# A planner that counts a longer time from a slot-list scatter to whatever rests on its landing, with its places set anew

## The chip, the cores and the metric

One core of one Trainium2 chip. The time is device microseconds of one execution; of the kernel before, three runs gave a median of 997.97 us (997.52 to 999.89).

## The reference

Sliding-window attention feeds a mixture of experts. q, k and v are [8, 8, 576, 64] (8 batches, 8 heads, 576 positions, width 64), float32.

```python
scores = q @ k.T / sqrt(64) - slope[h] * |i - j|      # only 0 <= i - j < 128
attn   = softmax(scores) @ v
x      = attn.transpose(0, 2, 1, 3).reshape(4608, 512)
noisy  = x @ w_gate + log1p(exp(x @ w_noise)) * noise   # [4608, 8]
top2   = the two largest of a row; weights = softmax over them
out[t] = sum over its two experts e of weight * (relu(x[t] @ w1[e]) @ w2[e])
```

w1 is [8, 512, 1024], w2 [8, 1024, 512], so each expert serves some 1152 of the 9216 (token, expert) pairs.

## The kernel before, in words

Attention runs batch by batch on TensorE, VectorE (bias and maximum), ScalarE (exponential, evictions) and GpSimd (selects of the window's blocks, L600 and L601). `rows` and `gate` then make a batch's token rows and its gate logits: `row_major` (L786 scales a row tile out of its bank, L794 and L797 store it to xs_dram), and in `gate` the heads' logits are scaled (L832, VectorE) and summed over the heads on GpSimd (L841, L842). `route(b)` chooses the two experts of each of the batch's tokens and gives every pair a slot in its expert's list: a small table `listed` of 80 lines of 64 numbers is built (L941, L942 on VectorE) and added into slots_dram by an indirect DMA that GpSimd issues (`scatter`, L1009), once for each batch. `gates_out` stores the gate values into xs_dram (L1069, L1073).

What reads the lists: expert 0's first 1024 slots are three early blocks (384, 384 and 256 tokens), which may start when batches 0 to 3, 0 to 5 and 0 to 6 are listed (`CUTS` has 3, 5 and 6). `first_ids` loads such a list on SyncE's queue (L1078), turns it into token numbers on VectorE (`clipped`: L1083, L1084, L1044), and GpSimd gathers the tokens (L1337); the rows are split into two half-precision parts, transposed by DMA (L1455), and go through the first expert product (L1463) and the second. The remaining blocks ("second wave") get their lists from `second_ids` (L1873 and on), the output rows are added into the result by scatters (L1724).

The order of the work is made ahead of the launch. `Order` plays the whole kernel through as strands that yield operations with a planned duration and a rank; an engine that is free in the plan takes the waiting operation of least rank, and emits it then. The order of emission is the order of each engine's queue on the chip, SyncE's DMA queue among them. A strand may also wait until a planned time (`yield order.now + 2.5`). The plan carries no semaphores: what waits for what on the chip follows from the data that instructions touch in the order of emission, so an access to slots_dram waits for the landing of every scatter to it that was emitted before. The ranks come from the constants at the top of the file (`SCATTER[b]`, `ROUTE[b]`, `FINE[...]` and so on); a batch is 20 on the scale of routing.

Three places in the plan count the time until a scatter has landed:

- in `route`, a scatter takes the one token of the ring `listing` first, and `landed_list` gives it back 2.1 us after the scatter's planned end: the next batch's scatter can't be emitted before;
- at the end of `route(b)`, 2.5 us behind `sent[b]` (the batch's gate values stored), an early block's list load may begin;
- in `second_ids`, 2.5 us before the lists of the second wave.

The scatter itself is planned at 1.2 us on GpSimd, and 0.2 us (`LAG`) are added behind each operation.

Of the kernel before, what the change touches and what calls it, by code (L numbers as in the profile page):

```python
# [40 lines left out]
WIDE, HALF = 512, 256  # L41
REST = CAP - 2 * WIDE
BLOCKS = tuple(((FROWS, c - FROWS),) if z < NF else ((0, WIDE), (WIDE, WIDE), (2 * WIDE, c - 2 * WIDE)) for z, c in enumerate(CAPS))
ZERO, EMPTY = -868.7, -2
LOAD = 1336.2
VALUES = 522.7
GATE = (586.3, 114.2, 10.8, 223.3, 430.5, 595.2, 1222.1, 914.0)
ROUTE = (342.7, 2091.0, 1245.6, 114.7, 453.4, 734.2, 1823.4, 1585.4)
SCATTER = (825.8, 1619.1, 1254.4, -2580.7, 356.1, -2057.0, -1202.6, 1165.8)
FFN0, FFN1 = -37.1, 674.3  # L50
WEIGHTS = (1547.8, 1129.9)
TOKENS = -408.2
FINE = (-269.6, -67.8, 591.7, 499.2, 364.6, 91.4, -84.0, -165.4, -508.6, -68.4, -409.6, 76.9, 124.7, -71.9, -108.9, -18.6, -921.6, 304.5, 493.5, 400.7, 136.3, 66.3, 526.5, 2.2, 234.2, -476.5, -453.8, -47.5, -184.4, -278.0, 410.0, 13.0, 37.2, 126.9, -246.8, 12.9, -248.7, 24.3, -130.2, 10.5, -211.1, 146.0, -91.2, -314.4, -30.9, 272.5, -306.7, -204.8, -795.2, 68.5, 336.3, -528.3, 344.2, 61.4, -456.9, 111.8, -186.5, -50.6, -10.3, -525.8, -189.2, 13.2, 55.1, 270.0, 177.0, -536.1, 113.3, 36.7, -51.7, -60.8, 589.7, -248.0, -73.3, -88.5, 652.2, -8.9, -517.4, 295.6, 24.0, -285.0, 895.7, 310.8, -678.8, -379.9, -384.9, -317.9, 31.8, 33.5, -239.2, -604.6, -100.3, -134.7, 154.5, -665.9, 43.3, 311.1, 207.6, -18.8, 338.4, -65.9, -144.2, -324.3, 36.8, 219.5, -55.9, -124.3, 200.0, -551.8, 229.5, 106.3, 1.0, 383.8, -156.7, -416.1, -291.1, -190.4, 45.4, -262.7, -141.2, 180.6, -150.6, -450.1, -201.8, 120.2, -203.1, -129.0, 273.6, 32.0, 96.8, -401.0, -263.6, 134.3, -151.3, 504.8, 21.3, -241.5, -6.7, -424.3, -701.9, 780.4, 28.0, 576.4, -208.7, 237.4, -534.3, 273.3, 215.7, 380.0, 228.8, -184.6, 104.7)
STAGE = (855.9, -105.9, 923.9, 172.5, -770.8, 1148.3, 1067.9, 742.9)
MIDDLE = 1144.0
RESULT = 1472.4
SIZES = (1334.5, 424.5, 1529.3)
SOON = -672.8
TIGHT = (1, 5, 7)
QUICK = (5, 7)  # L60
LATE = (2094.9, -890.9, 647.9, 1175.8, 179.1, -270.3, -892.6, -769.0, 507.2, -1321.9, -1248.3, -168.7, -2569.7, -1705.9, -1040.2)
LAG = 0.2
ADD, TWS = 0.34, 5
BEHIND = 11.7
TURN, MARGIN, LATE_BY = (0.3, 0.3), 1.0, 1.0
TURNED = 7e4
SLACK = 0.8
PACE, READ_BY, AHEAD = 1.1, 2.0, 297.8
HELD = 3
SWITCH, NEAR = 0.093, 39.0  # L70
TOP, SOFT, SPLIT = (1.25, 1.25, 0.76), (1.56, 1.56, 0.8), (0.85, 1.35, 0.85)
SP_COST = 0.45
DMA_RATE = 300e3
# [165 lines left out]
def attention_moe(ctx: ExitStack, tc: tile.TileContext, qk_, v, w_gate, w_noise, noise, w1, w2,  # L239
# [13 lines left out]
    order = Order()  # L253
# [100 lines left out]
    def masks():  # L354
# [17 lines left out]

        yield dve(0.14, FINE[0] + -40, lambda: nc.vector.tensor_scalar(ident, rel, 0.0, None, op0=OP.is_equal))
        yield dve(0.14, FINE[1] + -40, lambda: nc.vector.tensor_scalar(before, rel, 0.0, None, op0=OP.is_lt))
        yield dve(0.7, FINE[2] + -40, folded)
        yield dve(0.7, FINE[3] + -40, of_first)
        for g in range(NP):
            for h in (2 * g, 2 * g + 1):
                yield either(0.65, 0.45, FINE[4] + -20 + 5 * g, LATE[9], lambda e, h=h: bias_of(e, h))
            mark(biased[g])  # L380
# [75 lines left out]
    def loads():  # L456

        for k in range(PAIRS):
            rank = 5 * k - LOAD
            t = qks[k] = yield (qkr, FINE[5] + rank)  # L460
            left[k] = len(GROUPS)
# [6 lines left out]
    def all_values():  # L468
        for y in range(2 * B):
            rank = 10 * y - VALUES  # L470
            if y == 0:
# [167 lines left out]
    def unit(u):  # L639
        k, gr = units[u]  # L640
        blocks = GROUPS[gr]
        t = k * NQ + blocks[0]
        r0, r1, r2, r3, r4, r5, r6, r7 = (t + z for z in STAGE)
        last = gr == 2
# [66 lines left out]
    def weighing(k):  # L711
        b, g, y = k // NP, k % NP, k // 2
        t = k * NQ + 1
        r6, r7 = (t + z for z in STAGE[6:])
        yield parted[k]
# [26 lines left out]
    def rows(b, last, t):  # L742
# [3 lines left out]
        nr, nz = 64 if last else 128, len(blocks)  # L746
        rank = t - GATE[b]

# [25 lines left out]
    def row_major(b, i, xu, den, t, done):  # L774

        rank = t - GATE[b]
        rows = 64 if i == 4 else 128
# [27 lines left out]
    def gate(b, blocks, xu, den, t, done):  # L805


        rank = t - GATE[b]
        nz, i = len(blocks), blocks[0]
# [52 lines left out]
    def route(b):  # L862
# [4 lines left out]
        ln, pl = lp[:, 0], lp[:, 1]  # L867
        rank = 20 * b - ROUTE[b]
        V = nc.vector
# [141 lines left out]

        rank = 20 * b + SCATTER[b]
        yield (listing, FINE[63] + rank)
# [2 lines left out]
        yield sent[b]  # L1016
        mark(routed[b])
        mark(over)
        yield order.now + 2.5
        if b in CUTS:  # L1020
            yield from first_ids(first[CUTS[b]], b + 1, rank)

    listing = Ring([0])

    def landed_list():
        yield order.now + 2.1
        put(listing, 0)

    def first_ids(blk, cut, rank):
# [98 lines left out]
    def weight_rank(e, f):  # L1128

        return 1000 + step_of(e) + f - 4 if e else WEIGHTS[0] + WEIGHTS[1] * f  # L1130

# [100 lines left out]
    def say(e):  # L1232
# [6 lines left out]
        yield begun[e - 1]  # L1239
        yield Op((("SP", 1.5, SIZES[2] + step_of(e) - 1),), load)  # L1240
        mark(known[e])
# [296 lines left out]
    def copied(o, t, rank, end, done):  # L1538
        yield end
        yield either(0.33, 0.34, FINE[123] + rank - MIDDLE, LATE[8], lambda e: copy(e, o, t))  # L1540
        yield order.now + SLACK
        mark(done)

    def two_sums(c, y, rank, end, copies, done, u):
# [3 lines left out]
        both = c[:, 0:2].rearrange("p a b -> p (a b)")  # L1548
        yield dve(0.6, FINE[124] + rank - MIDDLE, lambda: nc.vector.tensor_tensor(both, y, both, op=OP.add))  # L1549
        yield order.now + SLACK  # L1550
        mark(done)
        yield dve(ADD, FINE[125] + rank - MIDDLE, lambda: nc.vector.tensor_tensor(c[:, 4], c[:, 0], c[:, 1], op=OP.add))
        mark(u)

    def last_sum(c, at, t, rank, end, ready_, done, whole):
        yield end
        yield ready_
        yield dve(0.34, FINE[126] + rank - MIDDLE, lambda: nc.vector.tensor_tensor(c[:, at], t, c[:, 0], op=OP.add))  # L1558
        put(hbr, whole)
# [68 lines left out]
    def downs(steps):  # L1628
        held = []
        for blk, f, rank in steps:  # L1630
            yield blk.h[f][0]
            if blk.wide:
# [8 lines left out]
                for j, r in blk.tiles:  # L1641
                    end = yield pe(1.3, FINE[136] + rank, lambda: mm2_wide(blk, f, j, [ev[2] for ev in ws]), False)
                    if f == 3:
                        spawn(result(blk, j, r, rank - RESULT, end))
                spawn(after(blk, f, None, end))
                continue
            if blk is second[-1] and f >= 8 - HELD:
                held.append((f, chunks[blk.e, f]))
                yield chunks[blk.e, f][1]
                if f == 7:  # L1650
                    for j, r in blk.tiles:
                        for z, ev in held:
                            end = yield pe(0.655, FINE[137] + rank, lambda: mm2(blk, z, j, r, ev[2]), False)
                        spawn(result(blk, j, r, rank - RESULT, end))
                    for z, ev in held:
# [20 lines left out]
            for j, r in blk.tiles:  # L1676
                end = yield pe(0.655, FINE[140] + rank, lambda: mm2(blk, f, j, r, ev[2]), False)
                if f == 7:
                    spawn(result(blk, j, r, rank - RESULT, end))
            spawn(after(blk, f, ev[2] if blk.last else None, end))  # L1680
# [61 lines left out]
    def first_tokens():  # L1742
        for z, blk in enumerate(first):
            yield from tokens(blk, ranks1[8 * z] - TOKENS)

# [113 lines left out]
        yield dve(1.3, 1130, starts)  # L1859

    def second_ids():
        yield order.now + 2.5
        for q, blk in enumerate(second):
            rank = 1000 + 8 * q - AHEAD
            t = blk.ix = blk.at = yield (ixr, FINE[148] + rank)
            v = lists2[q % 2]
            nt, rem = blk.n // 128, blk.n % 128
            yield known[blk.e]

            def load_ids():  # L1870
                if blk.e < EARLY:
                    r0 = blk.e * EROWS + blk.s0
                    nc.sync.dma_start(v[:, 0:nt], dram(slots, r0, [[1, 128], [128, nt], [1, 1]]))  # L1873
                    if rem:
                        nc.sync.dma_start(v[0:rem, nt], dram(slots, r0 + nt * 128, [[1, rem], [1, 1]]))
                    return
                one_ = slots.rearrange("(e l) c -> e (l c)", e=E)[bass.ds(said[blk.e], 1)]
                s1 = blk.s0 + nt * 128
                if nt:
                    nc.sync.dma_start(v[:, 0:nt], one_[:, blk.s0:s1].rearrange("o (a p) -> p a o", p=128))  # L1880
                if rem:
                    nc.sync.dma_start(v[0:rem, nt], one_[:, s1:s1 + rem].rearrange("o p -> p o"))

            def numbers_():
                if nt:
                    tokens_of(v[:, 0:nt, 0], t.bitcast(F32)[:, 0:nt], spare[:, 0:nt])
                if rem:
                    tokens_of(v[0:rem, nt], t.bitcast(F32)[0:rem, nt:nt + 1], spare[0:rem, nt:nt + 1])

            yield from move(1e4, rank, load_ids)  # L1890
            yield order.now + READ_BY
            yield dve(0.3, FINE[149] + rank, numbers_)
            mark(blk.ids)
            spawn(weights_back(blk, rank))
# [142 lines left out]
```

## Time and profile before

| | |
|---|---|
| median of 3 runs | 997.97 us (997.52 to 999.89) |
| the profiled execution's own time | 997.48 us |
| its span, first to last instruction | 995.7 us |
| mean granted TensorE clock | 0.988 |
| TensorE busy | 951.8 us (96%) |
| VectorE busy | 822.1 us (83%) |
| ScalarE busy | 569.0 us (57%) |
| GpSimd busy | 382.3 us (38%) |
| HBM read and written | 158 GB/s over the span |

Times in the trace are from the span's start; what lies outside the span is 1.8 us. Attention and routing end near 255 us, the expert products fill the rest. Engines are PE (TensorE), PEld (its weight loads), DVE (VectorE), ACT (ScalarE), POOL (GpSimd) and SP (SyncE, which issues most DMAs); POOLq or SPq is such an engine's own instruction queue. L1078 is line 1078 of the kernel. A bracket behind an instruction gives the idle time of its engine before it and what the profile takes for the release; where a wait was for several things the name can be the wrong one.

### The profile page before, as it was taken

The numbers are of one execution on the slowest core, as the hardware profiler recorded it, in microseconds if no ns is written. First come the engines' busy times: TensorE is split into PE (matmuls) and PEld (weight loads), VectorE is DVE, ScalarE is ACT, GpSimd is POOL, SyncE is SP. The second block draws the span as 40 slices with busy tenths as digits, with TensorE's granted clock in tenths as the row PEclk, the third lists the DMA queues.
The fourth block names the chain that finished last, engine by engine and source line by source line (L and its number), as shares of the span: only waits on it lengthen the run. The fifth ranks groups of instructions, "written<-read, shape, count | busy, mean of one in ns | idle before, by whom it ended". The sixth has DMA issues, their size and how long they took to land. (4 is left out here: it accounts for less than half of the span.)

```text
span 995.7 us, 25350 instructions
## 1 busy us (share of the span) xinstructions
PE 951.8 (96%) x9040; PEld 668.4 (67%) x9040; DVE 822.1 (83%) x2813; ACT 569.0 (57%) x1516; POOL 382.3 (38%) x567
## 2 busy tenths in 40 slices
PE   7999899878999999999999999999999999999996
PEld 5777676655556967596768576766767586667753
DVE  8989899888558898797889988989897898889520
ACT  8998789751445656355646454654555374546312
POOL 4456567676333223222342234323313223343013
PEclk9999999988999999999999999999999999999998
DMA  9785688788799897797887688868997989686124
GB/s 327 241 270 184 182 261 245 215 259 215 206 256 213 216 220 151 167 180 210 163 218 172 164 166 222 192 188 132 224 179 188 200 195 242 114 174 133 19 33 52
DMA packets 236976, 188.89 MB, mean 190 GB/s; under 512 B 147696, under 2 KB 190992, under 8 KB 236848
## 3 DMA queue, kind: packets, MB, share of 16 engines
q1 hardware_dynamic: 219504, 148.31, 56.4%
q0 software_dynamic: 17344, 38.94, 21.4%
q8 instruction: 72, 1.18, 0.5%
q14 instruction: 56, 0.46, 0.1%
HBM read 116.24 MB, written 40.71 MB: 158 GB/s over the span
## 5 line engine op out<-in xcount | busy, mean ns | idle before, releaser
L1724 POOL DMA_INDIRECT out_dram<-yo,ix x69 | 123.7, 1793 | 255.1 <-ACT yo L276 178.3
L1620 PEld LDWEIGHTS <-hh 128*128 128x128 f16 x896 | 85.3, 98 | 73.3 <-issue 0.3
L1588 ACT ACTIVATE hh<-bank 128x256 f16<-128x256 f32 (+8 forms) x116 | 40.1, 347 | 142.3 <-PE bank L1463 57.8
L1620 PE MATMUL bank<-w2ha,hh 128*128 128x512 f16 x288 | 109.2, 379 | 0.0
L1620 PE MATMUL bank<-w2la,hh 128*128 128x512 f16 x288 | 109.2, 379 | 0.0
L1620 PE MATMUL bank<-w2ha,hl 128*128 128x512 f16 x288 | 109.2, 379 | 0.0
L1337 POOL DMA_INDIRECT xg<-xs_dram,ix x34 | 41.9, 1231 | 162.4 <-DVE ix L1084 103.2
L563 ACT ACTIVATE p<-p,nm 128x128 f32<-128x128 f32 x256 | 99.1, 394 | 4.2 <-DVE nm L539 4.0
L1489 PEld LDWEIGHTS <-wth 128*128 128x128 f16 x896 | 87.2, 98 | 18.4 <-issue 2.5
L1620 PEld LDWEIGHTS <-hl 128*128 128x128 f16 x448 | 43.8, 98 | 52.8
L1588 ACT ACTIVATE hh<-c 128x256 f16<-128x256 f32 (+1 forms) x82 | 41.6, 520 | 57.7 <-DVE c L1558 54.2
L524 PE MATMUL bank<-qk 64*64 64x192 f32 (+2 forms) x1152 | 61.4, 327 | 9.6 <-DVE nm L539 5.0
L539 DVE CUSTOM_DVE_ANT_0 p<-bank,bias 128x128 f32<-128x128 f32 x288 | 67.1, 285 | 1.4 <-PE bank L577 1.2
L614 PE MATMUL bank<-pT,vraw 128*64 128x128 f32 (+1 forms) x640 | 59.1, 332 | 8.3 <-POOL pT L601 3.8
L1603 DVE SCALAR_TENSOR_TENSOR hl<-bank,hh 128x384 f16<-128x384 f32 (+8 forms) x88 | 31.2, 363 | 42.1 <-ACT hh L1588 35.1
L276 ACT ACTIVATE yo<-bank,gw 128x512 f32<-128x512 f32 (+6 forms) x56 | 38.3, 686 | 46.5 <-PE bank L1620 22.2
L1337 POOL DMA_INDIRECT xp<-xs_dram,ix x35 | 42.1, 1204 | 58.3 <-DVE ix L1084 27.5
L1293 ACT ACTIVATE mraw<-mraw 128x1024 f32<-128x1024 f32 x56 | 58.6, 1048 | 7.4 <-DMA mraw<-in_w_dram 7.4
L1463 PEld LDWEIGHTS <-w1ha 128*128 128x128 f16 x544 | 48.7, 98 | 20.3 <-issue 0.6
L276 ACT ACTIVATE c<-bank 128x256 f32<-128x256 f32 x94 | 35.0, 378 | 47.2 <-PE bank L1489 46.6
L1489 PE MATMUL bank<-xhe,wth 128*128 128x256 f16 x224 | 61.0, 273 | 0.8 <-DVE c L1549 0.4
L1489 PE MATMUL bank<-xhw,wth 128*128 128x256 f16 x224 | 61.0, 272 | 0.6 <-DVE c L1549 0.4
(349 smaller groups left out, 3178.3 us busy)
## 6 DMA issues: line engine op xcount, KB each, us to landing
raw<-in_w_dram SPq DMA_DIRECT2D x144, 256.0 KB
mraw<-in_w_dram SPq DMA_DIRECT2D x56, 512.0 KB
qk<-in_qk_dram SPq DMA_DIRECT2D x32, 576.0 KB
vraw<-in_v_dram SPq DMA_DIRECT2D x16, 640.0 KB
out_dram<-xg SPq DMA_DIRECT2D x10, 1024.0 KB
xs_dram<-x SPq DMA_DIRECT2D x72, 128.0 KB
out_dram<-yo,ix POOLq DMA_INDIRECT x69
xs_dram<-xg SPq DMA_DIRECT2D x1, 1024.0 KB
```

Of the source, the lines that this page charges most:

```text
L276: nc.scalar.activation(o, i, AF.Copy, **kw)
L524: nc.tensor.matmul(s[h][r * 64:r * 64 + 64, o:o + n_ * 64], qk[half, m * 64:m * 64 + 64], blocks_of(qk[half, QW:QW + S], first_, step, n_) ...
L539: nc.vector.tensor_tensor_reduce(out=o, in0=i, in1=by, scale=-0.125, scalar=3.0e38, op0=OP.add, op1=OP.min, accum_out=m)
L563: nc.scalar.activation(pv, pv, AF.Exp, bias=nm[:, z, h:h + 1], scale=-1.0, accum_out=den[:, i, 2 * g + h:2 * g + h + 1])
L614: nc.tensor.matmul(y, t[:, kb, hh:hh + D], w, start=m == 0, stop=m == len(lst) - 1)
L1293: yield act(us, FINE[81] + rank, lambda: nc.scalar.activation(v, v, sum_, accum_out=o))
L1337: nc.gpsimd.indirect_dma_start(out=o, out_offset=None, in_=xs[0:blk.rows], in_offset=bass.IndirectOffsetOnAxis(ap=blk.at[0:r, j:j + 1], ax ...
L1463: nc.tensor.matmul(t[:, 0:blk.n], wp[:, c], x[:, c, 0:blk.n], start=c == 0 and z == 0, stop=c == 3 and z == 2)
L1489: nc.tensor.matmul(t, wp[:, at + kc], xp[:, 2 * o + kc], start=not add and kc + z == 0, stop=kc + z == 3, skip_group_check=add)
L1588: nc.scalar.activation(o, i, AF.Relu)
L1620: nc.tensor.matmul(blk.y[j], h[:, cs], wp, start=a == 0 and z + m == 0, stop=a == 3 and z + m == 3)
L1724: ins = nc.gpsimd.indirect_dma_start(out=out, out_offset=bass.IndirectOffsetOnAxis(ap=blk.ix[0:r, j:j + 1], axis=0), in_=t[0:r], in_offset ...
```

## The change

The two 2.5 and the 2.1 above become 4.8. Beside that nearly all ranks get other values: every constant from ZERO to LATE that the diff shows, AHEAD and NEAR. Sizes, tiles, engines and operations are the same.

```diff
-LOAD = 1336.2
-VALUES = 522.7
-ROUTE = (342.7, 2091.0, 1245.6, 114.7, 453.4, 734.2, 1823.4, 1585.4)
-SCATTER = (825.8, 1619.1, 1254.4, -2580.7, 356.1, -2057.0, -1202.6, 1165.8)
-FFN0, FFN1 = -37.1, 674.3
+LOAD = 1312.0
+VALUES = 521.5
+ROUTE = (344.2, 2070.6, 1239.7, 114.7, 451.0, 720.1, 1799.0, 1587.4)
+SCATTER = (826.8, 1590.9, 1231.4, -2587.1, 341.2, -2034.5, -1202.9, 1158.6)
+FFN0, FFN1 = -37.3, 650.3
...
-STAGE = (855.9, -105.9, 923.9, 172.5, -770.8, 1148.3, 1067.9, 742.9)
+STAGE = (854.4, -105.9, 922.3, 177.9, -775.2, 1103.9, 1074.4, 742.1)
...
-PACE, READ_BY, AHEAD = 1.1, 2.0, 297.8
+PACE, READ_BY, AHEAD = 1.1, 2.0, 259.0
...
-SWITCH, NEAR = 0.093, 39.0
+SWITCH, NEAR = 0.093, 42.4
...
         yield sent[b]
         mark(routed[b])
         mark(over)
-        yield order.now + 2.5
+        yield order.now + 4.8
         if b in CUTS:
             yield from first_ids(first[CUTS[b]], b + 1, rank)
...
     def landed_list():
-        yield order.now + 2.1
+        yield order.now + 4.8
         put(listing, 0)
...
     def second_ids():
-        yield order.now + 2.5
+        yield order.now + 4.8
         for q, blk in enumerate(second):
```

The 151 values of FINE move in the same way, for example its first ones:

```diff
-FINE = (-269.6, -67.8, 591.7, 499.2, 364.6, 91.4, -84.0, ...
+FINE = (-269.0, -55.2, 568.8, 482.6, 393.2, 92.5, -99.1, ...
```

## Rows read from the trace of the kernel before

**Rows 1.** Windows: busy us (instructions) of each engine, granted clock, DMA share, GB/s.
```profile
0.00:250.00 250.00, 219.22 (x3382) 159.14 (x3383) 224.22 (x1248) 192.64 (x782) 152.96 (x337) 0.97 0.78 240
250.00:950.00 700.00, 696.58 (x5392) 487.80 (x5391) 590.00 (x1544) 368.32 (x717) 219.27 (x220) 1.00 0.82 181
```

**Rows 2.** The same windows view, in stretches of 10 us (PE, PEld, DVE, ACT, POOL).
```profile
90.00:100.00 10.00, 9.60 (x151) 7.04 (x147) 9.84 (x49) 6.38 (x31) 4.17 (x8) 1.00 0.57 180
100.00:110.00 10.00, 7.33 (x105) 5.39 (x103) 7.08 (x49) 6.51 (x29) 8.25 (x21) 0.83 0.64 169
...
200.00:210.00 10.00, 8.87 (x116) 6.34 (x116) 8.47 (x62) 5.61 (x18) 7.96 (x17) 0.66 0.99 314
...
220.00:230.00 10.00, 3.54 (x24) 2.00 (x26) 7.17 (x26) 0.66 (x2) 9.36 (x13) 0.69 0.74 191
...
250.00:260.00 10.00, 10.00 (x64) 5.55 (x63) 7.54 (x31) 5.07 (x12) 2.64 (x5) 1.00 0.89 266
```

**Rows 3.** Timeline of GpSimd, 90 to 104 us: start, us, instruction, idle before and releaser.
```profile
92.34 1.68 POOL L1009 DMA_INDIRECT slots_dram<-listed,line_of  x1 [0.33 <-DVE nm L539]
...
99.43 1.46 POOL L1009 DMA_INDIRECT slots_dram<-listed,line_of  x1 [5.37 <-DVE bank L545]
100.37 1.81 POOL L841 TENSOR_TENSOR lt<-lt 128x256 f32<-128x256 f32 x2
...
103.24 0.21 POOL L842 TENSOR_TENSOR lg<-lt 64x16 f32<-64x16 f32 x1
```

**Rows 4.** Timelines of ScalarE and of TensorE, near 104 us.
```profile
103.49 0.24 ACT L872 ACTIVATE u<-lg 128x40 f32<-128x40 f32 x1 [4.07 <-POOL lg L842]
...
104.26 1.05 PE L783 MATMUL bank<-ident,xul 128*64 128x128 f32 x4 [2.67 <-ACT pT L276]
```

**Rows 5.** Timeline of VectorE, near 96 us.
```profile
96.31 0.22 DVE L942 TENSOR_TENSOR listed<-listed,bank 80x64 f32<-80x64 f32 x1
96.45 0.68 DVE L832 TENSOR_TENSOR lt<-bank,den 128x512 f32<-128x512 f32 x1
```

**Rows 6.** Waits of SyncE's queue: us in total, times, longest.
```profile
SPq L1078 <- DMA slots_dram<-listed,line_of: 8.5, 2, 6.4
```

**Rows 7.** Timelines of GpSimd (the scatters) and SyncE (the queue), 180 to 198 us.
```profile
182.15 1.54 POOL L1009 DMA_INDIRECT slots_dram<-listed,line_of  x1 [0.18 <-issue]
...
190.95 1.44 POOL L1009 DMA_INDIRECT slots_dram<-listed,line_of  x1 [0.23 <-DVE rk L878]
...
188.47 0.38 SPq L475 DMA_DIRECT2D vraw<-in_v_dram  x1
188.90 1.32 SPq L1073 DMA_DIRECT2D xs_dram<-gd  x1
196.86 1.28 SPq L1078 DMA_DIRECT2D list<-slots_dram  x3
```

**Rows 8.** Timelines of VectorE, GpSimd and TensorE behind that list load.
```profile
199.91 0.16 DVE L1083 SCALAR_TENSOR_TENSOR ids<-list,spare 128x3 f32<-128x3 f32 x1 [3.33 <-DMA list<-slots_dram]
...
200.75 1.01 POOL L1337 DMA_INDIRECT xg<-xs_dram,cl  x1 [6.16 <-DVE cl L1044]
...
201.13 1.11 PE L577 MATMUL bank<-ident,p 64*128 64x64 f32 x15 [3.19 <-DVE x L786]
```

**Rows 9.** Timelines of GpSimd and SyncE: the last scatter, the third early list.
```profile
255.18 1.52 POOL L1009 DMA_INDIRECT slots_dram<-listed,line_of  x1 [3.90 <-DMA xs_dram<-gd]
...
260.16 0.81 SPq L1078 DMA_DIRECT2D list<-slots_dram  x2
```

**Rows 10.** Timelines of SyncE and TensorE: third block's last transpose and first product.
```profile
283.88 1.22 SPq L1455 DMA_TRANSPOSE xle<-th  x1
...
298.81 0.27 PE L1463 MATMUL bank<-xhe,w1ha 128*128 128x256 f16 x1
```

**Rows 11.** Timeline of TensorE: the first expert product.
```profile
236.72 0.33 PE L1463 MATMUL bank<-xhe,w1ha 128*128 128x384 f16 x1
```

**Rows 12.** Waits of TensorE, 0 to 300 us: in total, times, longest.
```profile
PE bank L524 <- DMA qk<-in_qk_dram: 4.6, 1, 4.6
```

More of the change, by code (lines that the diff above doesn't have):

```diff
@@ L43 @@
 BLOCKS = tuple(((FROWS, c - FROWS),) if z < NF else ((0, WIDE), (WIDE, WIDE), (2 * WIDE, c - 2 * WIDE)) for z, c in enumerate(CAPS))
-ZERO, EMPTY = -868.7, -2
-LOAD = 1336.2
-VALUES = 522.7
-GATE = (586.3, 114.2, 10.8, 223.3, 430.5, 595.2, 1222.1, 914.0)
-ROUTE = (342.7, 2091.0, 1245.6, 114.7, 453.4, 734.2, 1823.4, 1585.4)
-SCATTER = (825.8, 1619.1, 1254.4, -2580.7, 356.1, -2057.0, -1202.6, 1165.8)
-FFN0, FFN1 = -37.1, 674.3
-WEIGHTS = (1547.8, 1129.9)
-TOKENS = -408.2
-FINE = (-269.6, -67.8, 591.7, 499.2, 364.6, 91.4, -84.0, -165.4, -508.6, -68.4, -409.6, 76.9, 124.7, -71.9, -108.9, -18.6, -921.6, 304.5, 493.5, 400.7, 136.3, 66.3, 526.5, 2.2, 234.2, -476.5, -453.8, -47.5, -184.4, -278.0, 410.0, 13.0, 37.2, 126.9, -246.8, 12.9, -248.7, 24.3, -130.2, 10.5, -211.1, 146.0, -91.2, -314.4, -30.9, 272.5, -306.7, -204.8, -795.2, 68.5, 336.3, -528.3, 344.2, 61.4, -456.9, 111.8, -186.5, -50.6, -10.3, -525.8, -189.2, 13.2, 55.1, 270.0, 177.0, -536.1, 113.3, 36.7, -51.7, -60.8, 589.7, -248.0, -73.3, -88.5, 652.2, -8.9, -517.4, 295.6, 24.0, -285.0, 895.7, 310.8, -678.8, -379.9, -384.9, -317.9, 31.8, 33.5, -239.2, -604.6, -100.3, -134.7, 154.5, -665.9, 43.3, 311.1, 207.6, -18.8, 338.4, -65.9, -144.2, -324.3, 36.8, 219.5, -55.9, -124.3, 200.0, -551.8, 229.5, 106.3, 1.0, 383.8, -156.7, -416.1, -291.1, -190.4, 45.4, -262.7, -141.2, 180.6, -150.6, -450.1, -201.8, 120.2, -203.1, -129.0, 273.6, 32.0, 96.8, -401.0, -263.6, 134.3, -151.3, 504.8, 21.3, -241.5, -6.7, -424.3, -701.9, 780.4, 28.0, 576.4, -208.7, 237.4, -534.3, 273.3, 215.7, 380.0, 228.8, -184.6, 104.7)
@@ L54 @@
-STAGE = (855.9, -105.9, 923.9, 172.5, -770.8, 1148.3, 1067.9, 742.9)
[L55 to L58, printed above, removed]
+ZERO, EMPTY = -857.2, -2
+LOAD = 1312.0
+VALUES = 521.5
+GATE = (586.3, 113.9, 26.9, 200.0, 448.9, 600.9, 1223.1, 933.2)
+ROUTE = (344.2, 2070.6, 1239.7, 114.7, 451.0, 720.1, 1799.0, 1587.4)
+SCATTER = (826.8, 1590.9, 1231.4, -2587.1, 341.2, -2034.5, -1202.9, 1158.6)
+FFN0, FFN1 = -37.3, 650.3
+WEIGHTS = (1554.8, 1178.0)
+TOKENS = -434.4
+FINE = (-269.0, -55.2, 568.8, 482.6, 393.2, 92.5, -99.1, -166.4, -509.2, -68.8, -408.6, 72.4, 109.4, -69.4, -83.6, -18.6, -918.7, 304.2, 492.6, 383.7, 127.4, 59.8, 503.2, 2.2, 220.6, -456.1, -467.4, -49.1, -164.0, -278.0, 370.6, 12.3, 81.8, 127.6, -265.1, 12.9, -255.7, 3.1, -129.8, 0.7, -186.7, 145.8, -81.1, -314.4, -31.0, 206.5, -275.3, -226.3, -809.0, 67.5, 311.8, -524.9, 345.8, 66.8, -458.8, 111.2, -181.1, -56.5, 19.8, -502.0, -197.1, 20.3, 5.2, 270.0, 146.6, -529.6, 110.9, 61.7, -32.4, -33.4, 591.2, -237.5, -79.1, -44.4, 621.2, -6.6, -515.8, 298.1, 24.0, -300.5, 907.5, 310.8, -678.6, -384.7, -392.5, -262.7, 24.9, 32.7, -238.1, -604.5, -92.5, -125.8, 153.0, -663.5, 36.2, 281.8, 210.2, -15.3, 296.9, -59.9, -130.1, -324.9, 36.5, 214.1, -55.9, -107.2, 192.8, -551.9, 208.7, 65.1, 1.0, 383.8, -170.1, -414.0, -299.8, -196.5, 49.3, -286.0, -151.4, 180.8, -151.0, -403.1, -211.1, 120.5, -202.3, -149.2, 284.1, 23.9, 24.4, -394.2, -263.2, 89.8, -154.3, 509.6, 25.3, -232.4, -6.7, -421.6, -701.9, 780.5, 23.7, 572.2, -208.6, 246.0, -542.7, 280.7, 232.7, 381.8, 206.0, -193.0, 101.4)
@@ L59 @@
+STAGE = (854.4, -105.9, 922.3, 177.9, -775.2, 1103.9, 1074.4, 742.1)
+MIDDLE = 1141.9
+RESULT = 1487.2
+SIZES = (1360.4, 424.9, 1533.7)
+SOON = -654.8
 TIGHT = (1, 5, 7)
 QUICK = (5, 7)
-LATE = (2094.9, -890.9, 647.9, 1175.8, 179.1, -270.3, -892.6, -769.0, 507.2, -1321.9, -1248.3, -168.7, -2569.7, -1705.9, -1040.2)
+LATE = (2082.6, -896.6, 632.3, 1187.7, 137.0, -269.8, -843.0, -797.9, 507.6, -1324.0, -1233.0, -161.6, -2573.4, -1709.3, -1043.4)
 LAG = 0.2
```

## The prediction

> **What bounds the kernel now.** I read long windows first. From 0 to 250 us TensorE is busy 219.2 us (30.8 idle, mean granted clock 0.97), from 250 to 950 us 696.6 (3.4 idle) [rows 1]. So from 250 us on TensorE sets the pace, and time can go only in attention, gate and routing before it; what is saved there passes to the end if the first expert block starts as much earlier. Ten-microsecond windows show dips: 100 to 110 (TensorE 7.33 busy), 200 to 210 (clock 0.66), and 220 to 230 (3.54 busy), where the last batch drains [rows 2]. In front of the first, VectorE is busy 9.84 of 10; it is the next engine late in this stage, so a dip gives back at most what VectorE lost in it.
>
> Then I asked what the first two dips waited for. The **first** begins on GpSimd: batch 0's list scatter was issued from 92.34 to 94.02, the next one ran only at 99.43, and the sum over heads (L841, L842) stood behind it until 103.45 [rows 3]. ScalarE waited 4.07 us for that sum, its evictions came late, and TensorE stood 2.67 us [rows 4]. The profile names a VectorE line as the releaser of the second scatter; that was not it, since the scatter's own data (L942) was written by 96.53 [rows 5]. The landing is what is left, 5.41 us after the issue's end.
>
> The **second** is on the DMA queue: SyncE's list loads (L1078) waited for scatters 8.5 us in two waits, the longest 6.4 [rows 6]. The queue's record before the load ends at 190.22, the load goes at 196.86. The last scatter ahead of it is the one at 190.95, which is batch 4's: this L1078 loads the first block's list, which wants batches 0 to 3 alone, and batch 3's scatter was at 182.15 [rows 7]. So the landing took 196.86 - 192.39 = 4.47 us. VectorE, with the list's numbers at the head of its queue, stood 3.33 us until 199.91; GpSimd, with the gather at its head, 6.16 us; TensorE 3.19 us, until VectorE got to L786 behind the numbers [rows 8].
>
> A third wait, on the last early list: the load goes at 260.16, 3.46 us after batch 7's scatter ends [rows 9]. TensorE is busy all through 250 to 260 [rows 2].
>
> **The change part by part.** The planner costs a scatter at 1.2 us, adds 0.2, and let the next scatter come 2.1 us behind that, a list load 2.5 us behind the batch's stored gates. Both become 4.8. From a scatter's start the planned landing goes from 3.5 to 6.2 us; the three landings above are 7.09, 5.91 and 4.98 us from the start. The new figure lies among them, the old one below all. No instruction is added or taken away; only the order in the queues can differ.
>
> (1) *Next scatter, batches 0 and 1.* Counted from 92.34, the plan freed the second scatter at 95.84, before the heads' product was there (97.13, [rows 5]), so the scatter went first. With 6.2 us it is freed at 98.54, after 97.13, so the sum goes first: its 3.08 us (100.37 to 103.45) from 97.13 on end near 100.2, and ScalarE's wait of 4.07 us shrinks below 1. TensorE's 2.67 us goes; VectorE lost 2.92 us in that window [rows 2], so it permits this. Gain 2.7; bounds 0 (the scatter stays first) and 4.4 (with 1.7 us for the window's clock of 0.83). I leave the clock out: TensorE ran part of that window at the lower of its levels (1.2 GHz), but VectorE comes next. The closest pair after it is 8.8 us apart [rows 7], so nothing queues behind the longer hold.
>
> (2) *First list load and its numbers.* Both are planned 2.3 us later (4.8 - 2.5). But what the load truly waited for is batch 4's scatter, and nothing in the planner ties the load to that one. So the wait shrinks by 2.3, not to nothing: SyncE's 6.4 to 4.1, VectorE's 3.33 to 1.0, as other work is set ahead of them. Gain 2.3; bounds 0 and 3.3. The clock of 0.66 in 200 to 210 I again give nothing: VectorE is busy 8.47 there. The gather comes no earlier than now, since the landing doesn't.
>
> (3) *Second and third lists.* Of L1078's two waits one is the first list's and one the third's, so the second list waits for nothing. The third is 2.3 us later in the plan and about as late in truth as now; its last transpose is issued by 285.10 and its rows are first used at 298.81 [rows 10]. 13.7 us hide it: 0; with that cover gone it costs 2.3.
>
> (4) *Lists of the second wave* begin 2.3 us later in the plan, in a stretch where TensorE has no idle [rows 2]: 0, with the same 2.3 as the bound.
>
> (5) *Places.* Nearly every rank moves, mostly by less than 30 on a scale where a batch is 20. The trace can't show what that orders anew. Its bounds are, downward, the idle time outside the two dips, 30.8 - 5.9 = 24.9 us, and upward one more wait as long as the longest seen, 6.4 us. I take 0, as the 700 us that hold most of the moved work have 3.4 us of idle to lose or win.
>
> Sum: 2.7 + 2.3 = 5.0 us off the profiled execution's 997.48 gives 992.5. That execution is 0.5 below the median of 997.97, so the forecast is **993.0**.
>
> **A rule against it.** The Trainium skill, page "DMA: Bandwidth & Descriptors", section "Anatomy of one DMA — SWDGE (gpsimd) path", gives a GpSimd DMA about 2.0 us fixed, most of it the receipt of the write, and the bytes at 436 GB/s: an estimate of 2.05 us for this scatter of 80 x 64 floats. By that page the old figures would be right and the new ones some 2.7 too long. This trace's 3.46, 4.47 and 5.41 us behind the issue's end disagree.
>
> **Rivals.** *The landing is not what was waited for.* Then the holds only push: the first gather 2.3 us later and the first expert block with it, 997.97 + 2.3 = 1000.3. For it: the releaser printed at 99.43 is another line. Against: [rows 5, 7]. 0.05.
>
> *The second stop stays whole*, because the load is again put right behind batch 4's scatter and the numbers keep their place. Only (1) is gained: 995.3. For it: the reason given in (2). 0.13.
>
> *Taken back at the drain.* From 220 to 230 TensorE is idle 6.5 us: batch 7's last selects pass through a GpSimd that is busy 9.36, and the first block, which starts at 236.72, is not there to fill in [rows 2, 11]. If the gathers and transposes stay where they are, batch 7 ends sooner and TensorE waits longer for them: 998. 0.10.
>
> *More.* Both stops vanish (3.3 and 2.7), and GpSimd, which lost 6.16 us in front of the gather, has batch 7's selects done that much sooner, so the 6.5 us of idle in 220 to 230 go as well: 12.5 in all, so 985.5. 0.08.
>
> *The wait moves under a load that matters.* In the new order a load of q and k or of values is put behind the waiting list load on SyncE. Then the 6.4 us hold up the scores of a batch, as a late q and k did once near the start for 4.6 us [rows 12]; price 6.4, less the 2.7 of (1): 997.97 + 3.7 = 1001.7. It decides by one thing: whether L465 or L475 issues within 7 us behind L1078. One such load (L475) now stands at 188.47, just ahead of the wait [rows 7], so a shift of a few microseconds suffices. 0.24.
>
> **How the numbers follow.** The forecast (993.0, its own range 990 to 996) has 0.40; the others as given. About 0.3%, 3 us, is what a measurement of this kernel can tell from no change, so faster means below 995.0. Faster: 0.37 of the forecast's, all of *more*, 0.05 of the stop that stays: 0.50. Same: 0.03 of the forecast, 0.08 of that stop, the drain's 0.10, 0.04 of the pushed holds: 0.25. Slower: 0.24 and 0.01: 0.25. The range runs from 986.5 to 1002.5; about half of *more* and nearly half of the last rival lie outside, some 0.15.
>
> **What would show it.** Right: GpSimd runs L841 ahead of batch 1's scatter and that scatter's 5.4 us of idle is gone; TensorE's busy time in 100 to 110 is above 9; L1078's longest wait is near 4 us, the first list's numbers wait near 1; TensorE's idle before 250 us is near 26 us and the 700 us after it look the same. Wrong: the numbers still hold VectorE 3 us; the waits are gone but the first L1463 still starts at 236 to 237 us (drain); or TensorE waits for q and k after 150 us (the last rival). If the first L1463 comes 5 us sooner and the end does not, (5) is where it went.

## The result

The changed kernel is slower: ratio 1.0051 to the kernel before, 95% interval [1.0035, 1.0066] (medians 1002.11 and 997.5 us, 22 runs each); in a later session, beside two of the experiments, 1.0033 [1.0011, 1.0054]. The forecast was 993.0. The executions spread from 998.68 to 1007.92, and the profiled one took 1006.75 (span 1005.0), so its 9.3 us over the profiled one of before are more than the kernels' distance of 4.6 in the medians.

By windows (columns as in [rows 1]), the kernel after:

```profile
0.00:250.00 250.00, 221.12 (x3377) 158.50 (x3378) 224.06 (x1249) 194.32 (x789) 150.36 (x340) 0.96 0.77 240
250.00:950.00 700.00, 691.59 (x5333) 482.45 (x5331) 587.38 (x1534) 361.46 (x702) 213.77 (x210) 1.00 0.82 181
...
100.00:110.00 10.00, 9.92 (x175) 7.36 (x173) 9.89 (x68) 9.50 (x41) 8.65 (x23) 1.00 0.85 246
...
190.00:200.00 10.00, 5.62 (x111) 4.11 (x107) 4.52 (x41) 5.89 (x24) 7.96 (x13) 1.00 0.44 109
```

and one stretch of the kernel before that the prediction did not list:

```profile
190.00:200.00 10.00, 6.94 (x120) 4.84 (x114) 6.34 (x34) 8.39 (x37) 4.15 (x8) 0.99 0.54 152
```

The dip at 100 to 110 is gone ([rows 2] had TensorE 7.33, VectorE 7.08). In its place 190 to 200 is worse on TensorE and VectorE, and behind 250 us TensorE idles 8.4 us instead of 3.4.

**First stop.** Timelines of GpSimd and ScalarE, answering to [rows 3, 4]:

```profile
92.38 1.68 POOL L1009 DMA_INDIRECT slots_dram<-listed,line_of  x1 [0.32 <-DVE nm L539]
97.27 1.25 POOL L841 TENSOR_TENSOR lt<-lt 128x256 f32<-128x256 f32 x2 [3.21 <-DVE lt L832]
...
99.11 1.47 POOL L1009 DMA_INDIRECT slots_dram<-listed,line_of  x1 [0.16 <-issue]
...
101.58 0.24 ACT L872 ACTIVATE u<-lg 128x40 f32<-128x40 f32 x1 [0.17 <-POOL lg L842]
```

The sum over heads goes ahead of the second scatter, the scatter's 5.37 us of idle is 0.16, and ScalarE's 4.07 is 0.17. What was won lasts at least until batch 3's scatter, which goes at 179.60 (next fence) instead of 182.15.

**Second stop.** Waits of SyncE's queue, then timelines of SyncE, GpSimd, VectorE and TensorE, answering to [rows 6 to 8, 11]:

```profile
SPq L1078 <- DMA slots_dram<-listed,line_of: 12.9, 2, 7.5
...
185.64 0.48 SPq L1078 DMA_DIRECT2D list<-slots_dram  x1
193.73 0.81 SPq L1078 DMA_DIRECT2D list<-slots_dram  x2
194.58 0.47 SPq L1073 DMA_DIRECT2D xs_dram<-gd  x1
...
195.79 0.57 SPq L475 DMA_DIRECT2D vraw<-in_v_dram  x1
...
179.60 1.52 POOL L1009 DMA_INDIRECT slots_dram<-listed,line_of  x1 [0.38 <-DVE listed L942]
...
190.72 1.46 POOL L1009 DMA_INDIRECT slots_dram<-listed,line_of  x1 [4.14 <-DVE nm L539]
...
196.31 0.21 DVE L1083 SCALAR_TENSOR_TENSOR ids<-list,spare 128x3 f32<-128x3 f32 x1 [5.34 <-DMA list<-slots_dram]
...
198.56 0.17 PE L894 MATMUL bank<-both,before 128*128 128x8 bf16 x1 [2.93 <-DVE both L959]
...
237.65 0.33 PE L1463 MATMUL bank<-xhe,w1ha 128*128 128x384 f16 x1
```

The first list is three loads, one for each 128 slots. From the first one's start to the last one's end they take 8.90 us on SyncE, because the new order puts batch 4's scatter between the first and the second. The scatter, emitted behind the first load, waits for its landing (GpSimd idle 4.14 us; the releaser printed is a VectorE line, and the experiments `apart` and `apart_scatter` show that it was the load); the second load, emitted behind the scatter, waits for that landing. Both wait for nothing they need: before batch 4 is placed, expert 0's base is raised to a line's boundary (L901, L902), so that batch's lines are others than the list's. SyncE's longest wait is 7.5 us, not 4.1, VectorE's 5.34, not 1.0. The first expert product starts 0.9 us later than in [rows 11]; but in a second profiled execution of the changed kernel (`again`) it starts at 236.54, 0.2 us sooner, so by this sign the two kernels can't be told apart. Behind it they can: from 250 to 300 us TensorE is busy 49.40 us in the kernel before, 45.06 in the changed one and 47.34 in `again`.

**Third list.** It now waits 5.4 us for batch 7's scatter, which it doesn't need either (2.1 in the kernel before). Its load still goes sooner than in [rows 9], at 258.36 against 260.16. But VectorE, with the list's numbers at the head of its queue, now stands 2.96 us (0.74 before). Some 30 us later TensorE stands, and not for the third block's rows: it waits 1.40 us for ScalarE (L1588) and 3.02 us for VectorE (L1603), which move the hidden values of another block out of its banks. VectorE stands there for a list of the second wave, which SyncE loads at 290.71, behind the third block's transposes. Waits of SyncE's queue, 240 to 270 us, then timelines of SyncE, VectorE and TensorE:

```profile
SPq L1078 <- DMA slots_dram<-listed,line_of: 5.4, 1, 5.4
...
258.36 0.82 SPq L1078 DMA_DIRECT2D list<-slots_dram  x2
...
286.44 2.86 SPq L1455 DMA_TRANSPOSE xle<-th  x1
...
290.71 1.23 SPq L1880 DMA_DIRECT2D list<-slots_dram  x1
...
260.93 0.16 DVE L1083 SCALAR_TENSOR_TENSOR ids<-list,spare 128x2 f32<-128x2 f32 x1 [2.96 <-DMA list<-slots_dram]
...
292.04 0.16 DVE L1083 SCALAR_TENSOR_TENSOR ix<-list,spare 128x4 f32<-128x4 f32 x1 [3.07 <-DMA list<-slots_dram]
...
289.96 0.39 PE L1613 MATMUL bank<-w2ha,hh 128*128 128x512 f16 x1 [1.40 <-ACT hh L1588]
...
293.59 0.61 PE L1613 MATMUL bank<-w2ha,hl 128*128 128x512 f16 x1 [3.02 <-DVE hl L1603]
...
308.98 0.27 PE L1463 MATMUL bank<-xhe,w1ha 128*128 128x256 f16 x1
```

and of VectorE in the kernel before:

```profile
262.68 0.16 DVE L1083 SCALAR_TENSOR_TENSOR ids<-list,spare 128x2 f32<-128x2 f32 x1 [0.74 <-DMA list<-slots_dram]
```

### The profile page after: what moved, and what is told of

The parts are those of the page before. It is cut to its first block, busy times and chain, and to the rows that moved or that the text cites. A ratio compares the mean times of both kernels' runs of the same rounds, so it can differ in the third digit from the quotient of the medians.

```text
span 1005.0 us, 25350 instructions
## 1 busy us (share of the span) xinstructions
PE 957.5 (95%) x9040; PEld 668.7 (67%) x9040; DVE 823.0 (82%) x2812; ACT 568.2 (57%) x1517; POOL 378.4 (38%) x567
## 5 line engine op out<-in xcount | busy, mean ns | idle before, releaser
L1588 ACT ACTIVATE hh<-bank 128x256 f16<-128x256 f32 (+8 forms) x116 | 40.4, 350 | 150.1 <-PE bank L1463 91.0
L1588 ACT ACTIVATE hh<-c 128x512 f16<-128x512 f32 (+1 forms) x82 | 41.5, 518 | 56.7 <-DVE c L1558 56.4
L1489 PE MATMUL bank<-xle,wth 128*128 128x256 f16 x224 | 61.1, 273 | 0.0
L1489 PE MATMUL bank<-xhe,wtl 128*128 128x256 f16 x224 | 61.1, 273 | 0.0
```

Of the source, the lines that this page charges most:

```text
L1489: nc.tensor.matmul(t, wp[:, at + kc], xp[:, 2 * o + kc], start=not add and kc + z == 0, stop=kc + z == 3, skip_group_check=add)
L1588: nc.scalar.activation(o, i, AF.Relu)
```

## The experiments

Each ratio is to the kernel before, run on the same chip; below, the "times" of a plan are its two 2.5 and its 2.1.

**1. The change taken apart.** `hold_all` is the kernel before with three 4.8 and the old places; `hold_next`, `hold_list` and `hold_second` have one 4.8 each; `places` is the changed kernel with the old times. The three edits, with comments that the kernel doesn't have:

```diff
-        yield order.now + 2.5      # list load (hold_list)
+        yield order.now + 4.8
...
-        yield order.now + 2.1      # next scatter (hold_next)
+        yield order.now + 4.8
...
-        yield order.now + 2.5      # second wave (hold_second)
+        yield order.now + 4.8
```

`hold_all`: 

> The three waits of 4.8 us with the places of the kernel before (whose median was 997.5 us; the changed kernel's was 1002.1). Theory A, the split list load: the changed kernel loses where its first list's three loads lie around batch 4's scatter. Here the three stand together in front of that scatter, so ScalarE to TensorE stop less there and the gain of batch 1's later scatter stays: 993 to 996. Theory B, the new places lose time in the first expert blocks (260 to 310 us), whatever the lists do: without them nothing is lost there, 993 to 997. Theory C, the longer waits themselves cost time: 1000 to 1003, like the changed kernel.

`hold_next`: 

> Old places, and 4.8 us only for the next scatter; list loads keep 2.5. All theories expect GpSimd's 5.4 us of idle ahead of batch 1's scatter to go and TensorE to be above 9 of 10 busy from 100 to 110 us. If that gain of 2.7 us lasts to the end: 993.5 to 996. If it is taken back where the last batch drains: 997 to 998. Theory C for this wait: 999 or more.

`places`: 

> The new places with the old waits of 2.1 and 2.5 us. Theory A: the list loads stand together in front of batch 4's scatter here too, so the loss goes: 997 to 999 (batch 1's scatter again waits for its landing). Theory B: the loss stays, 1000 to 1004, with more than 2 us of TensorE idle between 260 and 310 us. Theory C: back to 997.

`hold_list`: 

> The kernel before with its places; only the hold ahead of an early list's load goes from 2.5 to 4.8, so the first list is still emitted behind batch 4's scatter. By the prediction's second step: SyncE's longest L1078 wait 4.1 instead of 6.4, VectorE's 1.0 instead of 3.33, 2.3 us gained, ratio 0.997 to 0.999. Rival, the places fit one plan only: what stands behind the hold is dealt anew (the orders of TensorE and VectorE differ over most of the run), the stop is shorter and the time 3 to 9 us longer all the same, ratio 1.003 to 1.009, as with all three holds.

`hold_second`: 

> The kernel before with its places; only the hold ahead of the second wave's lists goes from 2.5 to 4.8. The early lists and all scatters of the routing keep their order, so nothing changes before 250 us. By the prediction's fourth step 0: ratio 0.998 to 1.002. Rival, the places fit one plan only: the second wave's transposes and weight loads trade places on SyncE's queue and TensorE loses 2 to 5 us at 270 to 310; ratio 1.002 to 1.006.

| kernel | ratio | interval |
|---|---|---|
| hold_all | 1.0067 | [1.0042, 1.0091] |
| hold_next | 1.0099 | [1.0065, 1.0133] |
| places | 1.0172 | [1.0144, 1.0200] |
| hold_list | 1.0221 | [1.0202, 1.0240] |
| hold_second | 1.0334 | [1.0308, 1.0360] |

`hold_all` can't be told from the whole change (1.0051); the others are worse, `hold_next` narrowly. `hold_all` (median 1006.1 us) ended above all three expectations. `hold_next` did what was expected of it up to 110 us (TensorE busy 9.96 of 10), but only the expectation of theory C, that the longer waits cost time by themselves, held for its end, and that theory gave 997 for `places`, which took 1015.5. So neither the times nor the places are the loss by themselves. In `hold_all`, `hold_next` and `places` the first list's three loads stand in front of batch 4's scatter, and there the scatter waits for their landing: GpSimd stands 7.68, 3.67 and 5.83 us ahead of it.

`hold_list` tests step (2) of the prediction with the load kept behind batch 4's scatter. There VectorE's stop goes, as foretold: other work (L786 first) is set ahead of the numbers, and it reaches them at 200.12 without idle. SyncE's wait for the first list is 3.9 us (forecast 4.1, before 6.4); but `hold_second`, in which nothing is changed up to there, has 3.5, so this one figure shows nothing. Waits of SyncE's queue, 180 to 210 us, and a timeline of VectorE:

```profile
SPq L1078 <- DMA slots_dram<-listed,line_of: 3.9, 1, 3.9
...
200.12 0.16 DVE L1083 SCALAR_TENSOR_TENSOR ids<-list,spare 128x3 f32<-128x3 f32 x1
```

In this order, however, the second list is split round a scatter (two loads from 238.35, the third at 244.83), and the kernel is 2.2% slower; the rival expected at most 0.9%.

`hold_second` is the clearest: nothing is emitted otherwise before 250 us. (Its first expert block starts 2.1 us sooner than in the kernel before all the same, so that much can lie between two executions of one order.) From 350 to 950 us TensorE then stands 25.8 us, where the kernel before has 2.1; the rival had expected 2 to 5 us, at 270 to 310. Windows of `hold_second`, and its groups of TensorE from 350 to 500 us (line, shapes and count, then busy us and mean ns, then idle time ahead and what ended it):

```profile
350.00:500.00 150.00, 143.05 (x1043) 99.56 (x1041) 121.82 (x315) 78.24 (x145) 45.42 (x47) 0.99 0.87 181
500.00:650.00 150.00, 143.89 (x1138) 103.40 (x1136) 123.98 (x324) 78.37 (x146) 40.16 (x44) 0.98 0.78 168
...
800.00:950.00 150.00, 138.93 (x1141) 95.17 (x1138) 112.26 (x288) 84.81 (x161) 38.54 (x43) 0.98 0.82 166
...
L1489 PE MATMUL bank<-xle,wth 128*128 128x256 f16 x54 | 15.4, 286 | 2.0 <-DMA xle<-th 2.0
L1489 PE MATMUL bank<-xhe,wth 128*128 128x256 f16 x54 | 15.3, 284 | 2.7 <-DMA xhe<-th 2.7
```

The same windows of the kernel before:

```profile
350.00:500.00 150.00, 150.00 (x1109) 105.43 (x1107) 127.43 (x329) 82.93 (x161) 44.85 (x46) 1.00 0.85 183
500.00:650.00 150.00, 149.09 (x1187) 106.48 (x1186) 138.81 (x354) 81.39 (x157) 52.70 (x49) 1.00 0.82 190
...
800.00:950.00 150.00, 149.19 (x1250) 107.29 (x1248) 124.77 (x307) 75.38 (x151) 44.73 (x40) 1.00 0.68 140
```

2.3 us put into the plan deal out the whole second wave anew, and TensorE waits for token tiles that came in time before. So the ranks belong to one plan: the new places come to 1.0172 with the old times and to 1.0051 with the new ones, and no single part has a price that could be added to another's.

**2. The list loads.** `together` is the changed kernel with one list's loads emitted at the first one's place (the changed body of `fetch_ids`, which issues them in a loop, is left out here):

```diff
-            spawn(fetch_ids(ids[:, j], blk.s0 + j * 128, rank, fetched))
+            spawn(fetch_ids(ids, blk.s0, rank, fetched, nt if j == 0 else 0))
```

> The changed kernel, with the loads of one early list emitted together at the place of the first, so that no scatter lies between them; the plan is the same. Theory A: VectorE's wait for the first list's numbers falls from 5.3 us below 2, SyncE's 7.5 us wait goes, and the time falls by 3 to 5 us, to 997 to 999. Theory B: the wait falls too, but the time stays within 1.5 us of 1002.1, as the loss lies behind 260 us. Theory C: no change, 1002.

Ratio 0.9998 [0.9977, 1.0020]. Timelines of SyncE, GpSimd, VectorE and TensorE:

```profile
185.78 2.71 SPq L1078 DMA_DIRECT2D list<-slots_dram  x3
...
190.99 1.46 POOL L1009 DMA_INDIRECT slots_dram<-listed,line_of  x1 [4.28 <-DVE nm L539]
...
191.35 0.39 DVE L1084 SCALAR_TENSOR_TENSOR ids<-list,spare 128x3 f32<-128x3 f32 x1
...
233.96 0.33 PE L1464 MATMUL bank<-xhe,w1ha 128*128 128x384 f16 x1
```

VectorE's stop is gone, the first product starts 3.7 us sooner than in the changed kernel (2.6 sooner than in `again`), and half of one per cent is back, close to what theory A had. `apart` keeps the order and takes out the waits between an early list's loads and the scatters of later batches, both ways; `apart_before` does it to the kernel before (cut to the lines put in; comments added):

```diff
+            for z, (*_, cut) in enumerate(FIRST):
+                if b >= cut:      # the scatter does not wait for the loads
+                    tc.declare_no_dep(ins, group=f"list{z}", ...)
+                    tc.add_to_no_dep_group(f"late{z}", ins)
...
+            tc.declare_no_dep(ins, group=f"late{z}", ...)   # nor a load for them
+            tc.add_to_no_dep_group(f"list{z}", ins)
```

`apart`: 

> The changed kernel with its plan and order of emission; only the waits between an early list's loads and the scatters of later batches, which fill other lines of the slots, are taken out (both ways). Theory split: these waits are the 5.5 us that loading the three together gave back, and some more, since here no scatter waits for a load either: SyncE's L1078 wait of 7.5 us and GpSimd's 4.14 us before batch 4's scatter both go, VectorE's 5.34 before the list's numbers goes, the first L1463 starts near 232 to 233 us (237.65 in the changed kernel, 233.96 with the loads together), time 993 to 996. Rival, the longer waits of the plan themselves cost what is lost, through later gathers: the first L1463 stays at 236 to 238, time 1000 to 1003. If the time before 250 us comes back and the end does not (997 or more), what is left is lost at 275 to 300 us.

`apart_before`: 

> The kernel before with the same waits taken out. Theory: the first list's load no longer waits for batch 4's scatter (6.4 us on SyncE, 3.33 on VectorE, 6.16 on GpSimd before the gather), so the second stop of the kernel before goes without any longer hold: SyncE's wait near 1 to 2 us behind batch 3's scatter (which started at 182.15), the first L1463 at 232 to 234 us instead of 236.72, time 993 to 995. Rival, drain: batch 7's last selects set when GpSimd is free, the gathers only come to stand among them, TensorE's idle in 220 to 230 grows by what the stop gives, time 996 to 998.

`apart` has 0.9949 [0.9926, 0.9972], `apart_before` 0.9984 [0.9967, 1.0001]. Timelines of `apart`, the same engines (lines stand lower by the lines put in):

```profile
186.43 2.69 SPq L1084 DMA_DIRECT2D list<-slots_dram  x3
...
187.57 1.46 POOL L1009 DMA_INDIRECT slots_dram<-listed,line_of  x1 [0.23 <-DVE rk L878]
...
192.90 0.19 DVE L1093 SCALAR_TENSOR_TENSOR ids<-list,spare 128x3 f32<-128x3 f32 x1
...
231.97 0.33 PE L1473 MATMUL bank<-xhe,w1ha 128*128 128x384 f16 x1
```

No engine stands for the first list any more. `apart` beats both kernels; no other version that ran had a lower ratio. To the kernel before, those waits were worth 0.16%, with an interval that reaches from nothing to 0.33%; to the changed one 0.8% (against `again`) to 1.0%. That difference is more than the 0.3 to 0.5% by which the changed kernel is slower: the waits of no use are what turns its gain into a loss. `apart_before` gained less than was expected of it: its list load goes at 191.96, 4.9 us sooner, but its first product at 235.61 only 1.1 us sooner, which is nearer to the drain rival.

**3. Which side, which list.** `apart_load` frees only the loads (the two lines under the scatter's comment take no `declare_no_dep`), `apart_scatter` only the scatters; `apart_first` and `apart_third` free both sides for one list (`if z == 0`, `if z == 2`); `again` is the changed kernel beside the last two.

`apart_load`: 

> The changed kernel, its plan and order as they are; an early list's loads no longer wait for the scatters of later batches, but such a scatter still waits for a load that was emitted ahead of it. Both ways together gave a ratio of 0.9949 to the kernel before, neither 1.0051. If the loads' side is what costs: all three loads go near 186 us, VectorE's wait of 5.34 us before the list's numbers goes, batch 4's scatter still stands its 4.1 us on GpSimd (190.7), the first L1463 starts near 234 us as with the three loads together; ratio 0.996 to 1.000. If the scatter's side is what costs, ratio 1.003 to 1.006 here.

`apart_scatter`: 

> The same with the other side alone: batch 4's scatter no longer waits for the first list's first load, but the second load, emitted behind the scatter, still waits for its landing. If the loads' side is what costs: the scatter goes near 187.6 instead of 190.72, its landing near 193.5, the second load and VectorE's numbers with it, 3 us sooner than in the changed kernel (196.31); the first L1463 near 234.5; ratio 0.998 to 1.002, halfway. If the scatter's side holds the whole, the ratio is 0.995 as with both.

`apart_first`: 

> The changed kernel; the waits between list loads and later scatters are taken out for the first early list alone. Theory, two lists lose: the first list's share comes back, the first product of the first block starts at 232 to 234 us, but the third list's load still waits 5 us for batch 7's scatter, its last transpose still ends past 280 us and TensorE still has a hole at 275 to 295: ratio 0.998 to 1.001. Rival, the first list is all of it: ratio 0.994 to 0.996, as with the waits of all lists out.

`apart_third`: 

> The same for the third early list alone. Theory, two lists lose: up to 240 us as the changed kernel (the first product of the first block at 237 to 238 us), then the third list's load goes 4 us sooner, its last transpose ends 5 us or more sooner than 289 us and TensorE's 250 to 300 is busy above 48: ratio 0.999 to 1.002, about half of the 1.0% back. Rival, the third list is hidden as the prediction's third step had it: ratio 1.003 to 1.007, as the changed kernel.

`again`: 

> The changed kernel as it is, for the comparison on the same chip: ratio 1.0035 to 1.0066.

| kernel | ratio | interval | first product, us |
|---|---|---|---|
| apart_load | 0.9951 | [0.9937, 0.9966] | 234.87 |
| apart_scatter | 0.9993 | [0.9973, 1.0012] | 234.01 |
| apart_first | 0.9995 | [0.9974, 1.0017] | 230.43 |
| apart_third | 1.0002 | [0.9983, 1.0021] | 236.50 |
| again | 1.0033 | [1.0011, 1.0054] | 236.54 |

`apart_load` came out better than expected; it frees the third list too. Two lists lose: against `again`, freeing the first is worth 0.38% and freeing the third 0.31%. For the third it isn't the first product's start but a later hole. Windows from 270 to 295 us of the kernel before, the changed one, `again`, `apart_first`, `apart_third` and `apart`, a fence each:

```profile
270.00:295.00 25.00, 24.40 (x133) 12.70 (x132) 13.05 (x50) 12.08 (x25) 8.72 (x9) 1.00 1.05 258
```

```profile
270.00:295.00 25.00, 20.35 (x105) 10.31 (x106) 11.06 (x36) 7.47 (x15) 8.44 (x10) 0.94 1.19 182
```

```profile
270.00:295.00 25.00, 22.38 (x120) 11.36 (x119) 10.96 (x37) 9.04 (x18) 8.80 (x10) 1.00 1.13 230
```

```profile
270.00:295.00 25.00, 21.48 (x116) 10.91 (x114) 9.47 (x34) 10.57 (x21) 8.27 (x10) 1.00 1.25 224
```

```profile
270.00:295.00 25.00, 25.00 (x139) 13.31 (x137) 14.33 (x49) 12.27 (x24) 11.56 (x13) 1.00 1.14 261
```

```profile
270.00:295.00 25.00, 25.00 (x136) 13.15 (x135) 14.23 (x49) 12.94 (x25) 10.61 (x13) 1.00 1.15 247
```

Where the third list waits in the new order, TensorE loses 2.6 to 4.7 us of 25; where it is free, nothing. In `apart_third` the list's load goes at 252.27 and the third block's last transpose ends at 278.64, in the changed kernel at 258.36 and 289.30. That what TensorE lacked came late because SyncE's queue was held by these transposes is read from the traces; no run tested that link by itself.

**4. The output scatters.** In the changed kernel the DMA falls to some 100 GB/s from 280 to 290 us, where the first block's three output scatters (276.01 to 281.64) stand beside the third block's transposes (one of them 6.04 us long). `free_after` and `free_before` leave those scatters out:

```diff
             nc.gpsimd.memset(pad, 0.0)
+            if blk is first[0]:
+                return
```

`free_after`: 

> The changed kernel without the output scatters (L1724) of the first early block, so these 384 rows are left out of the result; everything else is issued in the same order. Theory places: in the changed order these three scatters stand next to the second wave's transposes at 276 to 290 us and take the DMA there (100 GB/s, transposes of 6.0 us, TensorE busy 45.06 of 50 in 250 to 300); without them TensorE is busy above 48 there and the time is 997 to 999, 3 to 5 below the changed kernel's 1002.1. Rival, the loss there comes from the gathers and mraw's loads, or TensorE simply catches up with late data: busy stays near 45 to 46, time 1001 to 1002.

`free_before`: 

> The kernel before without the same three output scatters (384 rows left out of the result). Theory places: in the old order they go at 270.65 to 274.48, ahead of the transposes, and cost TensorE nothing (49.40 busy of 50 in 250 to 300): time 996.5 to 997.5, within 0.1% of before. If it falls by as much as the changed kernel does without them, the scatters cost the same in both orders and aren't where the places lose.

Ratios 1.0037 [1.0022, 1.0051] and 1.0007 [0.9992, 1.0022]; the second is as expected. In `free_after` the hole is gone from 250 to 300 us (TensorE busy 49.95 of 50), but the time can't be told from the changed kernel's. The expectation of 997 to 999 fell: the scatters' nearness isn't what costs the time. The traces show that the loss moved: from 300 to 350 us `free_after` loses 2.04 us, the longest stop 1.51 us behind VectorE's L1603. Windows from 250 to 350 us of `again`, `free_after` and `apart_third`, a fence each:

```profile
250.00:350.00 100.00, 97.04 (x687) 63.30 (x685) 70.91 (x218) 47.17 (x91) 29.37 (x31) 1.00 0.95 213
```

```profile
250.00:350.00 100.00, 97.91 (x692) 64.29 (x691) 71.88 (x223) 47.52 (x92) 24.40 (x28) 1.00 0.90 208
```

```profile
250.00:350.00 100.00, 99.96 (x718) 66.55 (x717) 74.64 (x225) 49.73 (x97) 30.11 (x31) 1.00 0.96 220
```

Over the 100 us it wins 0.9 us on `again`; `apart_third` wins 2.9.

## Why the prediction was wrong

- *What bounds the kernel* held only where nothing behind 250 us is upset. `apart`'s first product starts 4.75 us sooner than in [rows 11], its 700 us from 250 on have 3.5 us of idle, and its profiled execution is 4.1 us shorter. But `apart_first`'s starts 6.3 us sooner, and its profiled execution is only 0.2 us shorter. That time can be lost only before 250 us was wrong: the changed kernel stands 5.0 us more behind it.
- *Step (1)* was right in mechanism: order, waits and window as foretold, and batch 3's scatter goes 2.55 us sooner (1.88 in `again`). What its 2.7 us is worth at the end was not measured, since `hold_next` upset the rest.
- *Step (2)* is where it failed first. Its premise stands: the load waited for batch 4's scatter, and nothing in the plan ties the two. From that I concluded that the load, put 2.3 us later, waits 2.3 us less. Where the load stays behind the scatter (`hold_list`) VectorE's stop does go. What follows from the premise is that the plan can put them in any order, one load ahead and two behind among them, and it did. [Rows 7] show three loads as one line, and I took them for one instruction; each is emitted by itself and can be cut off from the others. I also counted only the load's wait for the scatter, not the scatter's for a load. Nor is 4.8 us nearer to every landing than 2.1: the changed kernel's second load goes 1.55 us behind the end of batch 4's issue. The step was set at -2.3 and came out, by `together` and `apart_first`, a loss of some 4 to 5 us against the same plan without the split.
- *Step (3)* failed too: set at 0, as 13.7 us lie between the third block's last transpose and its first product. That cover did not go, it grew: in the changed kernel the last transpose ends at 289.30 and the first product is at 308.98, 19.7 us. The third list's wait costs the changed kernel some 3 to 5 us all the same (`again` against `apart_third`; `apart_first` against `apart`), on a path that the step left out: the list's numbers stand in VectorE's queue, and the block's transposes in SyncE's, ahead of what TensorE needs sooner for other blocks.
- *Step (4)*, 0 with a bound of 2.3, fails by itself: `hold_second` loses 3.3%. Its reason was read from 250 to 260 us of [rows 2], while these lists are loaded from 267 us on. In the changed kernel the new places cover it.
- *Step (5)*: the upper bound of 6.4 us, one more wait, was far too small for what a new dealing can do: the five kernels of part 1 lie 7 to 33 us above. That the changed kernel lost no more than it did is, as far as these runs show, the fitting of its places to its times. With the waits of no use taken out, the new plan gains 0.51%, much the 5.0 us of the sum; as `apart` also frees what stood before, the agreement is partly chance: against `apart_before` it is 0.35%.
- *Rivals.* The one that ended at 1001.7 came near in time, and its condition came true: L475 goes 1.2 us behind the waiting loads. But no instruction of TensorE waited for these values; the price fell on GpSimd and VectorE. The wait moved, but not under what I named, so that the time came near is luck. The rival by which the landing was not what was waited for is out at the second stop: where the loads alone are freed of the scatter (`apart_load`) they go one behind the other from 186.32 on.
- *The range* held 1002.1, near its upper end; 0.25 for slower was too little for a change that deals out a fitted order anew.

## What to carry to other kernels

When a plan knows nothing of the semaphores, look for every pair of accesses to one buffer that the new order could turn round, in both directions (a load behind a write, a write behind a load), and price each, one instruction at a time. Where the two touch other bytes, say so to the scheduler: that was worth 0.8 to 1.0% in the new order here, though hardly anything in the old one (0.16%). The new plan itself gained 0.35% once these waits were out. A cover read from the old order says nothing of the queues that the late work holds up on its way. Ranks fitted to one set of durations have a price only with that set; never judge a duration by changing it alone.

## What the runs showed of the hardware

- A list load of 128 numbers holds up a scatter behind it by its whole landing: 185.64 to 190.72 in the changed kernel, 4.7 to 5.1 us in five kernels with that order (the others are `again`, `apart_load`, `apart_third`, `free_after`), and 2.9 to 4.6 us from the last of three loads in `hold_next`, `places` and `hold_all`. A scatter's, from its start to the load behind it, was shorter there (190.72 to 193.73, 3.0 us) and longer in the kernel before (5.9 us).
- One scatter's landing varies between executions of the same order. Behind batch 4's scatter the load goes 4.47 us after the issue's end in the kernel before, 4.23 in `free_before`, 3.13 in `hold_second`, where VectorE's stop of 3.33 us shrinks to 0.42 though nothing up to there was changed. In the changed kernel's order it is 1.5 to 1.6 us in three kernels (the changed one, `again`, `apart_third`) and 3.07 in `free_after`. Timelines of SyncE and VectorE of `hold_second`:

```profile
195.59 1.28 SPq L1078 DMA_DIRECT2D list<-slots_dram  x3
...
198.64 0.16 DVE L1083 SCALAR_TENSOR_TENSOR ids<-list,spare 128x3 f32<-128x3 f32 x1 [0.42 <-DMA list<-slots_dram]
```

So a stop read from one profile, as [rows 8] were, can be nearly absent in the next execution.
